# Weight conversion with one integer addition on GpSimd in place of a power of two and a product with it

## The chip, the core and the metric

The kernel runs on one core of a Trainium2 chip. The metric is device time in microseconds (us), from the first to the last instruction, of executions of one fixed program. A core has five engines that each run their own instruction stream in order: TensorE (PE in the rows, its weight loads PEld), VectorE (DVE), ScalarE (ACT), GpSimd (POOL) and SyncE (SP), which here issues DMAs. Semaphores join the streams. An instruction that waits holds up everything behind it in its own stream.

## The reference

Attention with pooled queries (batch 4, 8 heads, 1152 keys, head size 64, pairs of queries averaged to 576), then a layer that mixes with a Fourier transform and has a two-matrix feed-forward part:

```
q_pool = q.reshape(B, H, S // 2, 2, D).mean(axis=3)
attn = softmax(q_pool @ k^T / 8);  x = attn @ v          # heads side by side: [4, 576, 512]
u = x + real(fft(fft(x, axis=1), axis=2))
un = (u - mean(u)) / sqrt(var(u) + 1e-6)
out = u + relu(un @ w_ch1) @ w_ch2                       # w_ch1 512x2048, w_ch2 2048x512
```

The two weight matrices come as float64. The core has no float64 arithmetic, so the kernel turns their bit patterns into float32 itself and splits each weight into a high part that the matmul format (float32r) holds exactly and a low part, the rest. Products are then summed as high x high, low x high and high x low (lines 718 to 720).

## The kernel before, in words

**Attention** goes over 16 pairs of heads, and in each over five blocks of queries, called units here. Lines 229 and 231: scores `s` (TensorE into PSUM) and their scaled copy with a running minimum into `sp` (VectorE). Line 243: exponential (ScalarE). Lines 256 and 259: `sp` transposed by TensorE, and copied out of PSUM to `pt` by ScalarE or, one in five, by VectorE. Line 272: `pt` times the values (TensorE). The next unit's scores are computed between the transposes of this one.

**Heads are prepared** one pair ahead: DMAs of `kr`, `qr`, `vs` from SyncE and of `ks` from GpSimd's queue (line 126), then on GpSimd the sum of query pairs `qr` (195) and the low part of the keys `ks` (198, four pieces), on ScalarE the high part of the queries `qh` (203), and on GpSimd their low part `ql` (206, two or three pieces). The scores of a head need all of these.

**Middle and feed-forward.** When a batch's eight heads are done, its Fourier transform (`dft`) and normalisation (`norm`) run in between, mostly on VectorE and ScalarE. In `norm`, `vt` (587 to 591) is the inverse deviation, `dg` (594) a diagonal of it, and the matmul of line 604 spreads it. `ffn` of a batch runs in blocks of 12 matmuls: four blocks of the first matrix (results `g`, high part on ScalarE in 737, low part on VectorE in 738), then four of the second, four times over. The first batch's blocks fill gaps between the attention's units, and at two places in the program (`drain`) the order demands that they are finished before the attention goes on.

**Weight conversion** is the part that changes. 32 tiles of 128 x 512 float64 are converted once by `convert`, one at a time past the list `inside`: load (SyncE, 643), absolute value of the upper word (ScalarE, 652), clamp (VectorE, 654), shift (VectorE, 656), the lower word scaled (ScalarE, 658), sign and bits joined into `wb` (VectorE, 662), power of two of its exponent (VectorE, 665), high part (ScalarE, 669), then on GpSimd, each in two halves of 128 x 256: lower word times power of two, difference of `wb` and the high part, and their sum as the low part (672). SyncE writes both parts to a DRAM tile (678), from which `wload` fetches them for every batch.

**What sets the order.** There is no scheduler at run time. A planner in the kernel keeps a clock `now`, and every `yield` or `after` says how many nanoseconds later the next step is written into the streams. So the numbers in the `yield`s fix where a step stands among its neighbours.

Of the kernel before, what the change touches and what calls it, by code (L numbers as in the profile page):

```python
# [12 lines left out]
F32 = mybir.dt.float32  # L13
F32R = mybir.dt.float32r
I32 = mybir.dt.int32
U32 = mybir.dt.uint32
AF = mybir.ActivationFunctionType
ALU = mybir.AluOpType
# [6 lines left out]
P = 128  # L25
# [29 lines left out]
def fused_kernel(ctx: ExitStack, tc: tile.TileContext, k2, q2, v2, w1, w2, cst, out):  # L55
    nc = tc.nc
# [10 lines left out]
    cvp = pool("cv", 1)  # L67
# [570 lines left out]
    going = []  # L638

    def convert(f, which):  # L640
        src = (w1, w2)[which]
        w = cvp.tile([P, 512, 2], I32, tag="wraw", name="wraw", bufs=3)
        nc.sync.dma_start(w, src[f].bitcast(I32).rearrange("p (c x) -> p c x", x=2))
        yield 6500 if going else 7000
        while inside:
            yield 400
        inside.append(f)
        high, low = w[:, :, 1], w[:, :, 0]
        a = cvp.tile([P, 512], F32, tag="cv", name="wa", bufs=4)
        ai = a.bitcast(I32)  # L650

        nc.scalar.activation(a, high.bitcast(F32), AF.Abs)
        yield 900 if going else 1400
        nc.vector.tensor_scalar(a, a, WORD_MIN, WORD_MAX, op0=ALU.max, op1=ALU.min)
        yield 700 if going else 1000
        nc.vector.tensor_scalar(ai, ai, 3, 0x3FFFFFF8, op0=ALU.logical_shift_left, op1=ALU.bitwise_and)
        rest = cvp.tile([P, 512], F32, tag="cv", name="rest", bufs=4)
        nc.scalar.activation(rest, low.bitcast(U32), AF.Copy, scale=2.0 ** -52)
        yield 700 if going else 1000
        t = cvp.tile([P, 512], F32, tag="cv", name="wb", bufs=4)  # L660
        b = t.bitcast(I32)
        nc.vector.scalar_tensor_tensor(b, high, -0x40000000, ai, op0=ALU.bitwise_and, op1=ALU.bitwise_or)

        yield 700 if going else 1000
        nc.vector.tensor_scalar(ai, b, -0x800000, None, op0=ALU.bitwise_and)  # L665
        yield 700 if going else 1000
        h = w.rearrange("p c x -> p (c x)").rearrange("p (x c) -> p x c", x=2)
        hi, lo = h[:, 0, :], h[:, 1, :]
        nc.scalar.copy(hi.bitcast(F32R), t)
        for o, x, y, op in ((rest, rest, a, ALU.mult), (t, t, hi.bitcast(F32), ALU.subtract), (lo.bitcast(F32R), t, rest, ALU.add)):  # L670
            for c in (slice(0, 256), slice(256, 512)):
                nc.gpsimd.tensor_tensor(o[:, c], x[:, c], y[:, c], op=op)  # L672
        if not going:
            yield 3000
        inside.pop()
        yield 3000 if going else 1500
        d = scw.tile([P, 2, 512], F32, name=f"w{which}_{f}")
        nc.sync.dma_start(d, h.bitcast(F32))
        wsc[which, f] = d
        yield 6500  # L680
# [7 lines left out]
    def converter():  # L688

        w, f = todo.popleft()  # L690
        g = convert(f, w)
        busy.append(f)

        def go():
            c = next(g, None)
            if c is not None:
                after(c, go)
            else:
                busy.pop()
        go()  # L700
# [257 lines left out]
```

## Time and profile before

| what | value |
|---|---|
| time, median of 3 runs | 1012.21 us (1011.35 to 1012.84) |
| span of the profiled execution | 1012.2 us |
| TensorE busy | 966.5 us (95%) |
| VectorE busy | 601.9 us (59%) |
| ScalarE busy | 526.5 us (52%) |
| GpSimd busy | 402.0 us (40%) |
| mean granted TensorE clock | 0.988 |

The profiled execution's own time is its span, 1012.2 us, the median of the runs to 0.01 us. Busy is the time in which an engine executes something; shares are averages over stages of different limits. The granted clock is the share of TensorE's full clock that the chip allowed, 1.00 for 2.4 GHz and 0.50 for 1.2 GHz.

### The profile page before, as it was taken

To read this page: it belongs to the slowest core of one execution; us is meant where nothing else is said; L and a number is where in the kernel's file an instruction comes from. 1 tells how busy PE (TensorE), PEld (TensorE's weight loads), DVE (VectorE), ACT (ScalarE), POOL (GpSimd) and SP (SyncE) were. 2 spreads that over 40 slices of the span, in tenths; PEclk is the share of its full clock that TensorE was granted. 3 is DMA by queue.
4 is the path that set the end of the run, shared out by engine and by line. 5 is a ranking of instruction groups with operands and counts; after the bars stand their busy time and mean duration, and the time that the engine had idled before them with its cause. 6 is when DMAs were issued, how large, how long until landed. Compare 5 with 4: busy or idle time off the path is not lost.

```text
span 1012.2 us, 19747 instructions
## 1 busy us (share of the span) xinstructions
PE 966.5 (95%) x7398; PEld 840.5 (83%) x7398; DVE 601.9 (59%) x1524; ACT 526.5 (52%) x1033; POOL 402.0 (40%) x583
## 2 busy tenths in 40 slices
PE   8999989898999998998999999999999999999998
PEld 5898878677788887776988888788888888899998
DVE  4557859889875597866544465745644275422222
ACT  5778869658865565655744454535744221301100
POOL 4555776868676667774523222222400000000000
PEclk7999989999999999999999999999999999999999
DMA  6545467556477875485655463254432544744342
GB/s 184 175 128 181 148 200 252 158 167 180 137 241 258 265 242 171 166 313 172 207 187 195 113 207 100 85 177 142 131 121 84 153 147 149 243 133 125 125 125 63
DMA packets 62515, 170.91 MB, mean 169 GB/s; under 512 B 16770, under 2 KB 20242, under 8 KB 62420
## 3 DMA queue, kind: packets, MB, share of 16 engines
q1 hardware_dynamic: 55924, 151.18, 47.1%
q0 software_dynamic: 4320, 17.70, 5.4%
q8 instruction: 58, 0.95, 0.4%
q10 hardware_dynamic: 2176, 0.79, 0.3%
q14 instruction: 37, 0.30, 0.1%
HBM read 146.88 MB, written 22.75 MB: 168 GB/s over the span
## 4 chain that ended last, share of the span: by engine, by line
PE 53%; DVE 2%; ACT 1%; DMA 1%; issue 1%; POOL 1%; SPq 0%; DVEq 0%; ACTq 0%; POOLq 0%
PE f L718 7%; PE f L720 6%; PE f L719 6%; PE s L229 6%; PE o L272 6%; PE t L256 5%; PE t L718 5%; PE t L719 5%; PE t L720 5%; DVE sp L231 1%; DMA w<-w 1%; PE f L532 1%; PE t L532 1%; ACT pt L259 0%; PE f L524 0%
## 5 line engine op out<-in xcount | busy, mean ns | idle before, releaser
L231 DVE TENSOR_SCALAR_CACHE_REDUCE sp<-s,bia 128x384 f32<-128x384 f32 x288 | 177.3, 615 | 89.0 <-PE s L229 66.3
L229 PE MATMUL s<-ks,qh 128*128 128x384 f32 x480 | 185.4, 386 | 12.5 <-DVE sp L231 3.9
L259 ACT COPY pt<-t 128x512 f32<-128x512 f32 (+2 forms) x243 | 125.0, 527 | 111.8 <-PE t L256 110.5
L243 ACT ACTIVATE sp<-sp,bia 128x1152 f32<-128x1152 f32 x144 | 180.1, 1255 | 3.2 <-DVE sp L231 2.8
L229 PE MATMUL s<-ks,ql 128*128 128x384 f32 x480 | 165.1, 344 | 2.9 <-POOL ql L206 2.5
L272 PE MATMUL o<-pt,vs 128*64 128x128 f32 (+1 forms) x2880 | 162.7, 266 | 1.0 <-DVE pt L259 0.8
L272 PEld LDWEIGHTS o<-pt,vs 128*64 128x64 f32 x2880 | 144.5, 138 | 22.8 <-issue 20.5
L256 PE MATMUL t<-ident,sp 128*128 128x128 f32 x1045 | 151.4, 277 | 7.2 <-ACT pt L259 3.0
L256 PEld LDWEIGHTS t<-ident,sp 128*128 128x128 f32 x1045 | 121.5, 141 | 27.8 <-issue 6.3
L198 POOL TENSOR_TENSOR ks<-kr,ks 64x288 fp32r<-64x288 f32 x120 | 99.1, 858 | 57.1 <-DMA ks<-in_k 23.5
L229 PEld LDWEIGHTS s<-ks,qh 128*128 128x128 f32 x480 | 92.6, 193 | 22.5 <-ACT pt L259 6.7
L229 PEld LDWEIGHTS s<-ks,ql 128*128 128x128 f32 x480 | 93.2, 194 | 4.2 <-POOL ql L206 2.9
L737 ACT ACTIVATE g<-f 128x512 fp32r<-128x512 f32 (+1 forms) x49 | 28.2, 576 | 120.2 <-PE f L720 120.2
L738 DVE SCALAR_TENSOR_TENSOR g<-f,g 128x512 fp32r<-128x512 f32 (+1 forms) x49 | 32.5, 663 | 97.1 <-ACT g L737 97.1
L206 POOL TENSOR_TENSOR ql<-qr,qh 128x288 fp32r<-128x288 f32 (+2 forms) x75 | 56.1, 771 | 77.9 <-ACT qh L203 76.8
L231 DVE TENSOR_SCALAR_CACHE_REDUCE sp<-s 128x384 f32<-128x384 f32 x144 | 78.6, 546 | 11.6 <-PE s L229 10.8
L718 PE MATMUL f<-g,w 128*128 128x512 f32 (+1 forms) x192 | 76.0, 396 | 2.0 <-PE f L604 1.0
L718 PE MATMUL f<-unh,w 128*128 128x512 f32 (+1 forms) x196 | 76.7, 391 | 0.9 <-DVE g L738 0.9
L672 POOL TENSOR_TENSOR rest<-rest,wa 128x256 f32<-128x256 f32 x64 | 50.4, 807 | 67.9 <-DVE wa L665 50.8
L720 PE MATMUL f<-unl,w 128*128 128x512 f32 (+1 forms) x196 | 74.6, 380 | 0.0
L719 PE MATMUL f<-unh,w 128*128 128x512 f32 (+1 forms) x196 | 74.3, 379 | 0.0
L720 PE MATMUL f<-g,w 128*128 128x512 f32 (+1 forms) x192 | 74.0, 385 | 0.0
(150 smaller groups left out, 1735.2 us busy)
## 6 DMA issues: line engine op xcount, KB each, us to landing
w<-w SPq DMA_DIRECT2D x128, 512.0 KB, 3.9
qr<-in_q SPq DMA_DIRECT2D x30, 576.0 KB, 4.4
ks<-in_k POOLq DMA_DIRECT2D x30, 576.0 KB, 6.3
wraw<-in_w SPq DMA_DIRECT2D x32, 512.0 KB, 3.5
w<-wraw SPq DMA_DIRECT2D x32, 512.0 KB, 2.6
vs<-in_v SPq DMA_DIRECT2D x32, 288.0 KB, 6.4
kr<-in_k SPq DMA_DIRECT2D x30, 288.0 KB, 6.8
out<-x SPq DMA_DIRECT2D x12, 256.0 KB, 2.0
```

The source lines that it names most:

```text
L198: nc.gpsimd.tensor_tensor(ks[D:, c], kr[D:, c], ks[D:, c].bitcast(F32), op=ALU.subtract)
L206: nc.gpsimd.tensor_tensor(ql[:, z], qr[:, 0, x:y], qh[:, z].bitcast(F32), op=ALU.subtract)
L229: nc.tensor.matmul(ps, lhsT=l, rhs=k, start=i == 0, stop=i == len(ops) - 1)
L231: nc.vector.tensor_scalar(sp[n, j][:, c], ps, -0.0625, bt[:, pc - 1:pc] if pc else None, op0=ALU.mult, op1=ALU.min, accum_out=bt[:, pc:pc ...
L243: last_exp[0] = nc.scalar.activation(t, t, AF.Exp, bias=bia.pop((n, j))[:, 2:3], scale=-1.0, accum_out=den[pr][:, col:col + 1]).ins
L256: nc.tensor.transpose(ps[:, i * P:i * P + P], sp[k][:, c * P:(c + 1) * P], ident)
L259: (nc.vector.tensor_copy if eng == "v" else nc.scalar.copy)(pt[:, :o], ps[:, :o])
L272: nc.tensor.matmul(po[y * D:y * D + D, :w], lhsT=qkv[2 * pr + y][3][:, c, :], rhs=pt[:, o:o + w], start=c == 0, stop=c == NKC - 1)
L672: nc.gpsimd.tensor_tensor(o[:, c], x[:, c], y[:, c], op=op)
L718: nc.tensor.matmul(ps, lhsT=ah, rhs=bh, start=first, stop=False)
L719: nc.tensor.matmul(ps, lhsT=al, rhs=bh, start=False, stop=False)
L720: nc.tensor.matmul(ps, lhsT=ah, rhs=bl, start=False, stop=last)
```

## The change

The rounding to float32 is done on the bit pattern. The lower word, scaled, is converted to an integer `k` by the ScalarE step that used to write `rest`, and GpSimd adds it to the joined bits as a 32-bit integer. So `wb` and `rest` go, with the power of two and with GpSimd's product with it; the difference of the sum and its high part is the low part directly. Per tile GpSimd has four halves in place of six, VectorE three instructions in place of four, ScalarE three as before. ScalarE's copy to the high part now follows a GpSimd instruction, where it followed VectorE's line 662, and the planned distances change.

```diff
         a = cvp.tile([P, 512], F32, tag="cv", name="wa", bufs=4)
+        k = cvp.tile([P, 512], I32, tag="cv", name="wk", bufs=4)
         ai = a.bitcast(I32)
...
-        rest = cvp.tile([P, 512], F32, tag="cv", name="rest", bufs=4)
-        nc.scalar.activation(rest, low.bitcast(U32), AF.Copy, scale=2.0 ** -52)
+        nc.scalar.activation(k, low.bitcast(U32), AF.Copy, scale=2.0 ** -29)
         yield 700 if going else 1000
-        t = cvp.tile([P, 512], F32, tag="cv", name="wb", bufs=4)
-        b = t.bitcast(I32)
-        nc.vector.scalar_tensor_tensor(b, high, -0x40000000, ai, op0=ALU.bitwise_and, op1=ALU.bitwise_or)
-
+        nc.vector.scalar_tensor_tensor(ai, high, -0x40000000, ai, op0=ALU.bitwise_and, op1=ALU.bitwise_or)
         yield 700 if going else 1000
-        nc.vector.tensor_scalar(ai, b, -0x800000, None, op0=ALU.bitwise_and)
-        yield 700 if going else 1000
+        halves = (slice(0, 256), slice(256, 512))
+        for c in halves:
+            nc.gpsimd.tensor_tensor(ai[:, c], ai[:, c], k[:, c], op=ALU.add)
+        yield 2300
         h = w.rearrange("p c x -> p (c x)").rearrange("p (x c) -> p x c", x=2)
         hi, lo = h[:, 0, :], h[:, 1, :]
-        nc.scalar.copy(hi.bitcast(F32R), t)
-        for o, x, y, op in ((rest, rest, a, ALU.mult), (t, t, hi.bitcast(F32), ALU.subtract), (lo.bitcast(F32R), t, rest, ALU.add)):
-            for c in (slice(0, 256), slice(256, 512)):
-                nc.gpsimd.tensor_tensor(o[:, c], x[:, c], y[:, c], op=op)
+        nc.scalar.copy(hi.bitcast(F32R), a)
+        for c in halves:
+            nc.gpsimd.tensor_tensor(lo[:, c].bitcast(F32R), a[:, c], hi[:, c].bitcast(F32R), op=ALU.subtract)
         if not going:
-            yield 3000
+            yield 1000
```

TensorE's stream keeps its order, but for the small matmuls of line 584 in the second batch's `norm`, which stand one feed-forward block (12 matmuls) earlier. The other streams move. Line numbers of the changed program are one or two off from those of before from here on: its 664 is the integer addition, 668 the high part, 670 the difference, 653 the absolute value, 735 the `g` of line 737.

GpSimd's stream where the head pair 8 and 9 is prepared, before; `wa`, `wb`, `rest`, `wraw` belong to the conversion, the others to the heads:

```order
L126 DMA ks<-in_k 128x1152
L672 TENSOR_TENSOR rest<-rest,wa 128x256 x2
L672 TENSOR_TENSOR wb<-wb,wraw 128x256 x2
L672 TENSOR_TENSOR wraw<-wb,rest 128x256 x2
L137 MEMSET qh 128x64
L138 MEMSET ql 128x64
L195 TENSOR_TENSOR qr<-qr 128x288 x2
L198 TENSOR_TENSOR ks<-kr,ks 64x288 x4
```

The same place in the changed program:

```order
L126 DMA ks<-in_k 128x1152
L664 TENSOR_TENSOR wa<-wa,wk 128x256 x2
L137 MEMSET qh 128x64
L138 MEMSET ql 128x64
L195 TENSOR_TENSOR qr<-qr 128x288 x2
L198 TENSOR_TENSOR ks<-kr,ks 64x288 x4
L670 TENSOR_TENSOR wraw<-wa,wraw 128x256 x2
```

Two of the six halves now stand ahead of the head's `qr`, and two behind its `ks`.

ScalarE's stream at the first `drain`, in the second batch's `norm`, before (`vt`, `dg`, `unh` belong to `norm`, `g` to the first batch's feed-forward blocks, `wa`, `rest` and `wraw` to the last conversions):

```order
L652 ACTIVATE wa<-wraw 128x512
L737 ACTIVATE g<-f 128x512
L658 ACTIVATE rest<-wraw 128x512
L737 ACTIVATE g<-f 128x512 x2
L669 CAST wraw<-wb 128x512
L652 ACTIVATE wa<-wraw 128x512
L589 ACT_TABLE_LOAD
L589 ACTIVATE vt<-vt 96x6
L658 ACTIVATE rest<-wraw 128x512
L594 ACTIVATE dg<-ident,vt 96x96 x6
L737 ACTIVATE g<-f 128x512
L669 CAST wraw<-wb 128x512
```

The same place in the changed program:

```order
L658 ACTIVATE wk<-wraw 128x512
L589 ACT_TABLE_LOAD
L589 ACTIVATE vt<-vt 96x6
L594 ACTIVATE dg<-ident,vt 96x96 x6
L668 CAST wraw<-wa 128x512
L653 ACTIVATE wa<-wraw 128x512
L658 ACTIVATE wk<-wraw 128x512
L735 ACTIVATE g<-f 128x512
L668 CAST wraw<-wa 128x512
L653 ACTIVATE wa<-wraw 128x512
L658 ACTIVATE wk<-wraw 128x512
L735 ACTIVATE g<-f 128x512
```

Conversions stand about one tile later against the feed-forward blocks. The last two `g` of this quarter stand, among the rows shown, behind one and two high parts of conversions (668), where they stood behind none and one (669).

## Rows read from the trace of the kernel before

**Rows 1.** Stretch of the conversions: its length, each engine's busy time, granted clock, DMA.

```profile
88.00:475.00 387.00, 354.90 (x2933) 298.80 (x2933) 301.29 (x727) 259.92 (x513) 277.25 (x382) 0.98 0.63 205
```

**Rows 2.** Two stretches at the lower clock, columns PE, PEld, DVE, ACT, POOL, clock, DMA.

```profile
137.20:144.00 6.80, 5.14 (x30) 4.30 (x32) 3.50 (x8) 4.45 (x9) 4.82 (x7) 0.50 0.48 184
181.60:184.90 3.30, 3.30 (x13) 3.13 (x13) 2.75 (x7) 1.05 (x3) 3.30 (x6) 0.50 0.00 0
```

**Rows 3.** Instructions on the tile wa: duration in ns, least, median, most; first and last start.

```profile
L672 POOL TENSOR_TENSOR rest<-rest,wa x64: 719/734/1269, 94.4 to 469.5; 128x256 f32<-128x256 f32 x64
L652 ACT ACTIVATE wa<-wraw x32: 662/676/703, 87.8 to 460.5; 128x512 f32<-128x512 f32 x32
L654 DVE TENSOR_SCALAR wa<-wa x32: 407/667/1075, 90.0 to 462.8; 128x512 f32<-128x512 f32 x32
L656 DVE TENSOR_SCALAR wa<-wa x32: 412/430/1030, 92.7 to 464.4; 128x512 int32<-128x512 int32 x32
L662 DVE SCALAR_TENSOR_TENSOR wb<-wraw,wa x32: 672/691/1296, 93.1 to 466.0; 128x512 int32<-128x512 int32 x32
L665 DVE TENSOR_SCALAR wa<-wb x32: 405/424/1042, 93.9 to 467.9; 128x512 int32<-128x512 int32 x32
```

**Rows 4.** Timeline of POOL and ACT, 118 to 122 us: start, length, what, [idle before].

```profile
118.54 3.28 POOL L198 TENSOR_TENSOR ks<-kr,ks 64x288 fp32r<-64x288 f32 x4 [4.47 <-issue]
119.18 0.60 ACT L669 CAST wraw<-wb 128x512 fp32r<-128x512 f32 x1
121.33 0.59 ACT L259 COPY pt<-f 128x512 f32<-128x512 f32 x1 [0.32 <-PE f L256]
```

**Rows 5.** Timeline of POOL, ACT and PE, 130 to 138 us.

```profile
130.57 1.43 POOL L672 TENSOR_TENSOR rest<-rest,wa 128x256 f32<-128x256 f32 x2
136.43 0.76 ACT L203 CAST qh<-qr 128x512 fp32r<-128x512 f32 x2 [3.59 <-POOL qr L195]
137.90 1.12 PE L256 MATMUL f<-ident,sp 128*128 128x128 f32 x4 [2.80 <-ACT pt L259]
```

**Rows 6.** Timeline of POOL, ACT and PE, 167 to 182 us.

```profile
167.55 0.83 POOL L126 DMA_DIRECT2D ks<-in_k  x1
176.15 3.80 POOL L198 TENSOR_TENSOR ks<-kr,ks 64x288 fp32r<-64x288 f32 x4 [6.02 <-issue]
177.79 0.27 ACT L280 COPY x<-o 128x128 f32<-128x128 f32 x1 [1.95 <-PE o L272]
181.40 0.59 PE L229 MATMUL s<-ks,ql 128*128 128x384 f32 x1 [2.53 <-POOL ql L206]
```

**Rows 7.** Timeline of ACT and PE, 225 to 227 us.

```profile
225.34 0.77 ACT L203 CAST qh<-qr 128x512 fp32r<-128x512 f32 x2 [2.83 <-POOL qr L195]
226.85 0.41 PE L229 MATMUL s<-ks,qh 128*128 128x384 f32 x1 [1.21 <-issue]
```

**Rows 8.** Timeline of POOL, ACT and PE, 374 to 385 us.

```profile
374.69 1.79 POOL L672 TENSOR_TENSOR rest<-rest,wa 128x256 f32<-128x256 f32 x2 [6.27 <-DVE wa L665]
381.90 0.76 ACT L203 CAST qh<-qr 128x512 fp32r<-128x512 f32 x2 [4.41 <-POOL qr L195]
384.41 0.44 PE L256 MATMUL t<-ident,sp 128*128 128x128 f32 x2 [2.23 <-ACT pt L259]
```

**Rows 9.** Timeline of DVE and PE, 245 to 248 us.

```profile
245.43 0.91 DVE L665 TENSOR_SCALAR wa<-wb 128x512 int32<-128x512 int32 x1
247.89 0.44 PE L229 MATMUL s<-ks,qh 128*128 128x384 f32 x1 [2.54 <-DVE sp L231]
```

**Rows 10.** Timeline of ACT, DVE and PE at the first drain, 436 to 461 us.

```profile
436.43 0.67 ACT L652 ACTIVATE wa<-wraw 128x512 f32<-128x512 f32 x1 [5.68 <-DMA wraw<-in_w]
453.93 0.15 DVE L587 TENSOR_SCALAR vt<-f 96x6 f32<-96x6 f32 x1
459.29 0.75 PE L604 MATMUL f<-dg,onesm 96*128 96x288 f32 x2 [1.25 <-DVE g L738]
461.00 0.47 PE L718 MATMUL f<-g,w 128*128 128x512 f32 x1 [0.95 <-PE f L604]
```

## The prediction

> **What bounds the kernel now.** I read the page first: TensorE is busy 95% of the span, and the chain of waits that ended last is mostly TensorE. So a change elsewhere can only move TensorE's idle time and its clock. Then the busy time by stretches, for the stretch in which weights are converted: in 387.0 us TensorE works 354.9, VectorE 301.3, POOL 277.3, ScalarE 259.9 [rows 1]. The most to be had there is thus 387.0 - 354.9 = 32.1 us, besides the clock. The first conversion starts at 87.8 and the last at 460.5 [rows 3]; behind them nothing but the order of a few instructions changes, and TensorE's stream is the same, so what is won or lost by then is passed on to the end. Third, TensorE's timeline with its waits: the 32 us lie in many gaps, and five of 1.2 to 2.8 us carry the argument. For each I looked at the streams of the engine it waits for, one step further back.
>
> In four of them the end of the chain is GpSimd, because six halves of a conversion stand ahead of a head's work. At 137.90 TensorE has waited 2.80 us for ScalarE, which had waited 3.59 us for `qr` on GpSimd, which came behind conversion halves that began at 130.57 [rows 5]. At 181.40 it has waited 2.53 us for `ql`; GpSimd was late since `ks` came 8.6 us after its DMA, and that DMA's issue stood behind a conversion until 167.55 [rows 6]. At 226.85 and 384.41 the pattern of 137.90 repeats, with 1.21 and 2.23 us [rows 7, 8]. The fifth, 2.54 us at 247.89, is VectorE's: a power of two of 0.91 us stands just ahead of the score copy that TensorE needs [rows 9]. The first two are also followed by the lower clock, 0.50 for 6.8 and 3.3 us, in which TensorE worked 5.14 and 3.30 us [rows 2].
>
> **The change part by part, removed work.** GpSimd loses 64 of 192 halves of 0.734 us, 47 us, and VectorE 32 powers of two of 0.424 us, 13.6 us [rows 3]. Little of that lies on TensorE's path; it counts where a gap stands.
>
> *Gap at 137.90.* Four halves of this conversion leave the place ahead of `qr`: 4 x 0.734 = 2.9 us, so `qh` could start near 133.5 in place of 136.43 [rows 5]. Against it stands a new wait earlier. The conversion before has its addition behind `ks`, which ends at 118.54 + 3.28 = 121.82 [rows 4]; the addition then ends near 123.3. ScalarE's high part, which ran at 119.18 for 0.60 us, now stands just ahead of the copy of 121.33 and waits for it, so that copy starts near 123.9 less the 0.6 us that its old place gives back: 2.0 us lost. ScalarE, free at 136.43 - 3.59 = 132.84 before, then comes to `qh` near 132.84 + 2.0 and with hand-overs at 135.2, behind GpSimd's 133.5. Net of both: 136.43 - 135.2, 1.2 us won.
>
> *Gap at 181.40.* GpSimd reaches the DMA of `ks` at least 2.9 us earlier (four halves), which covers the 2.53 us. But the high part now stands ahead of the copy of 177.79 and needs an addition that is queued behind `ql`; ScalarE was idle 1.95 us there [rows 6], so I take 1.0 us of new wait. Net 1.5 us.
>
> *The clock.* If neither gap is long, neither fall comes: half of 5.14 and half of 3.30 us, 2.6 and 1.6 [rows 2]. The first place keeps some idle time from the new wait, so I take 2.0 there. Together 3.6 us, from 0 to 4.2.
>
> *Gaps at 226.85 and 384.41.* At the second, GpSimd's idle 6.27 us for the power of two is over too, since its conversion now stands behind the head's `ql` [rows 8]. I take both whole: 1.2 + 2.2 = 3.4 us.
>
> *VectorE.* The power of two stood ahead of a score copy at 247.89, 0.9 us [rows 9]; for all its other places I count its usual 0.424 once [rows 3]: 1.3 us. Its 0.91 in place of 0.424 was a collision. The Trainium skill (SBUF — State Buffer, Who interferes with whom) has VectorE and GpSimd lock one pair of ports for a whole instruction, so that the loser blocks. The trace agrees, the shift ran 412 to 1030 ns [rows 3]. By that rule fewer GpSimd halves would free other VectorE steps too, and this term would be nearer 2 us and the sum below 0.7 lower; as heads' halves fill GpSimd's place there, I leave it at 1.3.
>
> **New instructions.** ScalarE's conversion to an integer takes the place of one step of its kind and counts nothing; ScalarE works 259.9 of 387 us, so a tenth of a microsecond more is covered, and without that cover 32 x 0.1 is 3 us. The trace has no integer addition on GpSimd. Below stands the float half, 719 ns at its fastest, above the slowest, 1269 [rows 3]. I take the median, 0.734, as it reads and writes operands of the same number and size as the float half that it replaces. The Trainium skill (GPSIMD Engine Reference, Elementwise — side-by-side cycle accounting) puts the floor of a two-input operation at its read port, about 2.6 cycles an element, which for 256 elements with its dispatch comes to an estimate of 0.71 us whatever the operation. By that the rival on the slow addition would hardly exist; no run here has shown it, so it keeps a chance.
>
> **The drain, where the change costs.** Before, conversions ran one tile ahead of the feed-forward blocks; now the last ones stand among the `g` and the normalisation [order rows of ScalarE]. The line: the sign step of one conversion stands in VectorE's stream behind 587, which ended at 454.08 [rows 10]. With ScalarE's 5.68 us wait for a weight load gone (the conversion concerned now comes later) and line 584 a block earlier, that end comes up to 2 us sooner, 452. From there, in order and each waiting for the one before: sign 0.69, addition 2 x 0.734, high part 0.60, then a loop of absolute value 0.68, clamp 0.67, shift 0.43, sign 0.69, addition 1.47, high part 0.60, then once more 0.68 + 0.67 + 0.43 + 0.69, and the low part of the last `g`, some 0.69 [rows 3, 4]. That is 2.76 + 4.54 + 2.47 + 0.69 = 10.5, and with about 0.1 for each of some ten hand-overs 11.5: 463.5. The same `g` released TensorE's line 604 at 459.29 before [rows 10], so the block that began at 461.00 begins 4.2 us later. What is behind: TensorE itself, with blocks and attention; nothing gives it back. From below 1.5 us, if only one loop is exposed; from above 9, if a third loop and another fall of the clock come on top.
>
> **Sum.** 1.2 + 1.5 + 3.6 + 3.4 + 1.3 = 11.0 us won. Where a gap closes, the next late engine often holds a part of it; VectorE is busy 301 of 387 us. I leave a quarter, and win 8.2. Less 4.2: 4.0. From 1012.2 that is **1008.2**, and the profiled execution is the median of the runs.
>
> **The rivals.**
> *Gaps refill.* VectorE at 78% is just behind, so half or less is won and the drain takes it: 5 - 4.2, about 1011.5. For it speaks that VectorE ends gaps of its own; against, that four of the gaps are plainly GpSimd's.
> *The drain decides (slower).* A further loop of 4.5 us is exposed, since the block's weights, written only behind the difference, come late as well, and the longer idle time brings a fall of the clock: 4.2 + 4.5 + 0.6, 9.3 lost against 6 won: 1015.5. It decides from where the block of 461.00 loses more than the 8.2 won ahead of it. For it speaks that conversions now stand a tile later; against, that two of the loops overlap TensorE's block of 2.7 us.
> *A slow addition (slower).* At 1269 ns a half, each loop in the drain and each of the two new ScalarE waits grows by 1.1 us: 2 x 1.1 and some 2.2 with it, 4 to 5 us, and the gains shrink by a like part: 1014. It decides from about 1.2 us a half.
> *All gaps close and the drain costs little.* 11.0 less 1.5: 1002.7.
>
> **How the numbers follow.** Forecast 0.44, gaps refill 0.18, the drain decides 0.16, a slow addition 0.07, all close 0.15. Changes under 0.2%, 2 us, can't be told from none. Faster by more: all of "all close", nearly all of the forecast and little of the refill, 0.60. Same: most of the refill and an edge of the forecast, 0.18. Slower: 0.22. The range, 1000 to 1015, holds "all close" with some room and the slow addition, and cuts the drain's rival in half. The forecast's own range is 1004 to 1010.
>
> **What would show it.** Right: in the profile after, GpSimd busy some 47 us less, VectorE some 14; no wait of ScalarE for `qr` over 2 us near 135, 225 and 380; `ks` DMA of the gap at 181 issued 3 us or more earlier; clock 1.00 there; an idle stretch of TensorE at the drain ahead of lines 604 and 718 longer by some 4 us. Wrong: an integer half well over 0.74 us; ScalarE waiting for the addition in more than three or four places; gaps of the old size with VectorE named.

## The result, and the profile after

The changed kernel takes 1002.75 us (median of 4 runs, 1001.70 to 1006.21) against 1012.27 us on the same chip: a ratio of 0.9908, 95% interval 0.9887 to 0.9928, so 9 us faster. Timed again, beside the experiments, it took 1005.44 us (6 runs, 1000.56 to 1006.23), ratio 0.9911, 0.9892 to 0.9930. The forecast was 1008.2 with a range of 1000 to 1015: right in direction and range, with a gain of 4 forecast where 9 came. The first profiled execution, with a span of 999.9 us, is one of the shortest of these runs; the second, 1003.8 us, lies nearer to the median. The experiments are compared with 1005.44. Both profiles are read below, because what differs between them turned out to be a cost of the change. In every run from here on the time is 1.7 to 2.1 us above the span. By that measure the profiled execution of the kernel before, with a span of 1012.2 us, took some 1014 us; it is then not the median of the first runs, as the section on before says, but near that of the later ones (1013.3 to 1014.0). The differences of starts below are taken against it.

From the page of the changed kernel: busy time, share of the span and instructions of each engine.

```profile
PE 965.2 (97%) x7398; PEld 840.3 (84%) x7398; DVE 578.7 (58%) x1492; ACT 527.0 (53%) x1033; POOL 351.8 (35%) x519
```

Busy time in the stretch of the conversions, to be held against [rows 1]; columns as there.

```profile
88.00:475.00 387.00, 365.60 (x3070) 309.05 (x3070) 286.06 (x720) 269.68 (x531) 229.69 (x322) 0.98 0.66 212
```

GpSimd (POOL) does 50.2 us less (402.0 before) and VectorE (DVE) 23.2 less, where 47 and 13.6 were forecast from medians. By sums the 32 powers of two took 16.6 us (0.52 on the mean), and the three steps that VectorE keeps take 6.1 us less than before: the clamp 2.8, the shift 1.9 and the sign step 1.5. TensorE works 365.6 of the 387 us, so in this execution its idle time there fell from 32.1 to 21.4 us. The mean granted clock of the stretch is 0.98, as before. The instructions on the tile wa, duration least, median, most:

```profile
L664 POOL TENSOR_TENSOR wa<-wa,wk x64: 713/728/1256, 93.4 to 455.2; 128x256 int32<-128x256 int32 x64
L670 POOL TENSOR_TENSOR wraw<-wa,wraw x64: 719/733/1244, 96.8 to 457.4; 128x256 fp32r<-128x256 f32 x64
L655 DVE TENSOR_SCALAR wa<-wa x32: 408/465/998, 89.3 to 450.5; 128x512 f32<-128x512 f32 x32
L660 DVE SCALAR_TENSOR_TENSOR wa<-wraw,wa x32: 672/690/1182, 92.4 to 453.7; 128x512 int32<-128x512 int32 x32
L668 ACT CAST wraw<-wa x32: 602/618/632, 96.1 to 456.0; 128x512 fp32r<-128x512 f32 x32
```

The integer half takes 0.728 us where 0.734 was taken: the rival of a slow addition is dead at once. That the prediction's estimate of 0.71 us comes close is luck: it added a dispatch time that is not GpSimd's. The Trainium skill (GPSIMD Engine Reference, Elementwise — side-by-side cycle accounting) gives a dispatch of about 156 ns for VectorE only; its 2.6 cycles an element for a two-input addition on GpSimd alone come, at 1.2 GHz, to an estimate of 0.55 us for 256 elements. The measured 0.728 us lies above that.

To see where the time went, I matched TensorE's instructions before and after by their count among those on the same tiles and took the start after minus the start before, in us. A column is an instruction, named by its start before; a negative number says how far the kernel is ahead there. First and second are the two executions of the changed kernel, the rest are the experiments below (late_3500 is late_early_3500).

```
start before   119.9 145.4 174.6 182.5 186.9 201.8 226.9 247.9 265.3 345.2 384.6 441.5 461.0 466.1   end
first            0.2  -5.4  -6.1  -8.7  -9.0  -9.9 -11.6 -14.3 -10.9 -12.8 -14.9 -16.7 -12.5 -12.2 -12.3
second           0.6  -4.5  -5.7  -7.7  -2.4  -4.4  -6.2  -7.5  -7.1  -8.9 -11.0 -12.8  -8.6  -8.4  -8.4
no_product      -1.2  -5.4  -6.0  -6.9  -6.6  -8.4  -9.4  -9.5  -9.6  -9.5 -11.8 -13.7 -13.7 -14.2 -13.7
six_halves      -0.8  -5.5  -5.0  -7.6  -4.0  -6.1  -7.6  -9.7  -5.7  -6.5  -8.2 -10.1  -5.4  -5.2  -5.3
power_back       0.9  -5.0  -4.6  -7.2  -6.4  -7.3  -8.7  -9.4  -7.3  -8.5 -10.9 -13.2  -7.5  -7.6  -7.5
split_order      0.8  -3.7   2.2  -0.9  -1.3  -2.4  -3.8  -3.6  -1.5  -2.6  -3.7  -2.1   5.8   5.1   9.0
short_drain      0.3  -5.0  -6.0  -8.6  -6.5  -8.6 -10.3 -12.0  -9.8 -11.0 -13.8 -15.4 -15.6 -16.4 -15.8
own_high        -0.8  -5.6  -6.4  -8.9  -9.2 -10.1 -11.8 -14.1 -12.0 -13.7 -16.5 -19.3 -15.9 -14.0 -11.9
late_high       -2.4  -8.8  -7.5  -9.8 -10.1 -10.2 -12.0 -14.5 -13.9 -14.9 -17.1 -19.0  -5.5  -3.2  -0.5
late_early      -0.0  -6.0  -2.0  -5.1  -1.7  -3.9  -5.7  -5.6  -2.6  -3.9  -7.3  -8.4 -12.6 -10.8  -8.3
late_3500       -0.3  -6.2  -5.3  -7.8  -3.7  -5.4  -7.1  -7.5  -4.2  -6.1  -9.0  -9.9 -13.9 -11.9 -10.6
short_own       -0.3  -5.6  -6.0  -8.6  -8.8  -9.8 -11.5 -13.3 -12.8 -13.7 -16.5 -19.1 -19.2 -20.1 -19.6
pool_high        0.0  -4.2  -4.6  -7.1  -7.4  -7.3  -9.0 -10.7 -10.5 -12.3 -14.8 -17.8 -17.7 -18.9 -18.9
```

In the first two lines: up to the drain 16.7 and 12.8 us are won, in many places; from 441.5 to 461.0 4.2 are given back, in both. The two executions part between 182.5 and 186.9, by 5.6 us; 3.0 of these come back by 265.3, where the first execution loses 3.4 us and the second 0.4.

**The place of 137.90 [rows 5].** Timeline of the changed kernel (first execution; POOL, ACT and PE), 110 to 137 us:

```profile
110.17 0.57 POOL L126 DMA_DIRECT2D ks<-in_k  x1
114.75 3.72 POOL L198 TENSOR_TENSOR ks<-kr,ks 64x288 fp32r<-64x288 f32 x4 [2.24 <-issue]
118.55 1.41 POOL L664 TENSOR_TENSOR wa<-wa,wk 128x256 int32<-128x256 int32 x2
...
121.02 0.63 ACT L668 CAST wraw<-wa 128x512 fp32r<-128x512 f32 x1
132.43 0.61 ACT L668 CAST wraw<-wa 128x512 fp32r<-128x512 f32 x1
132.93 0.77 ACT L203 CAST qh<-qr 128x512 fp32r<-128x512 f32 x2
...
136.44 0.44 PE L256 MATMUL f<-ident,sp 128*128 128x128 f32 x2 [0.69 <-ACT pt L259]
```

The 2.80 us of idle TensorE are 0.69, and ScalarE's copy of `qh` starts at 132.93 in place of 136.43, without its wait. The new wait that I put at 121 is not there: `ks` starts at 114.75, 3.8 us before its place in [rows 4], so the addition ends at 119.96, before ScalarE comes to its high part at 121.02.

**The place of 181.40 [rows 6].** Here the new wait came. The first execution (POOL, ACT and PE):

```profile
168.51 2.61 POOL L206 TENSOR_TENSOR ql<-qr,qh 128x288 fp32r<-128x288 f32 x3
171.09 1.93 POOL L664 TENSOR_TENSOR wa<-wa,wk 128x256 int32<-128x256 int32 x2
173.05 0.62 ACT L668 CAST wraw<-wa 128x512 fp32r<-128x512 f32 x1 [2.69 <-POOL wa L664]
174.94 0.44 PE L229 MATMUL s<-ks,qh 128*128 128x384 f32 x1 [0.56 <-ACT pt L259]
```

and the second:

```profile
168.49 4.67 POOL L198 TENSOR_TENSOR ks<-kr,ks 64x288 fp32r<-64x288 f32 x4 [4.55 <-DMA ks<-in_k]
173.25 2.44 POOL L206 TENSOR_TENSOR ql<-qr,qh 128x288 fp32r<-128x288 f32 x3
175.65 1.62 POOL L664 TENSOR_TENSOR wa<-wa,wk 128x256 int32<-128x256 int32 x2
177.30 0.62 ACT L668 CAST wraw<-wa 128x512 fp32r<-128x512 f32 x1 [6.18 <-POOL wa L664]
179.17 0.69 PE L229 MATMUL s<-ks,qh 128*128 128x384 f32 x1 [3.75 <-ACT pt L259]
```

with its busy time by a stretch, columns as in [rows 2]:

```profile
175.00:185.00 10.00, 6.25 (x52) 5.29 (x51) 7.03 (x21) 5.95 (x13) 5.05 (x9) 0.66 0.49 155
```

The chain reads from top to bottom: GpSimd waits 4.55 us for the DMA of `ks`; `ql` and then the addition stand behind; ScalarE's high part waits 6.18 us for the addition, and the copies of `pt` that stand behind it on ScalarE come late for TensorE, which idles 3.75 us and is then granted the lower level, 1.2 GHz. In the first execution `ql` starts 4.7 us earlier and the same chain costs 0.56 us, with no fall of the clock. That is the 5.6 us by which the two part here, and about the spread of the runs. The DMA of `ks` was issued at 156.22 in the first execution and at 158.30 in the second, and `ks` began 8.0 and 10.2 us later: half of the difference is the issue, half the way from there.

**The clock.** The two falls of before, at 137.2 and 181.5, are gone in the first execution, but others came, at 238.6, 436.5 and 446.8 (columns as in [rows 2]):

```profile
238.60:242.00 3.40, 3.37 (x26) 2.93 (x28) 2.02 (x6) 3.38 (x7) 3.40 (x5) 0.50 0.58 178
436.50:439.90 3.40, 3.40 (x10) 2.62 (x9) 0.42 (x2) 3.28 (x9) 2.41 (x4) 0.51 0.75 298
446.80:453.60 6.80, 6.46 (x14) 4.30 (x14) 6.73 (x11) 4.40 (x7) 2.68 (x4) 0.50 0.72 243
```

Before, the falls at 137.2, 181.5 and 461.4 put TensorE at the lower level for 13.6 us between 88 and 475 us. In the first execution after it is 13.6 us again, and in the second too (from 178.2 and from 447.9). The falls moved; they did not become fewer in time.

**The drain [rows 10].** PE, first execution:

```profile
434.98 0.64 PE L584 MATMUL f<-onesm,sq 128*96 128x1 f32 x6 [1.44 <-DVE sq L579]
442.65 0.65 PE L604 MATMUL f<-dg,onesm 96*128 96x288 f32 x2
447.10 1.33 PE L604 MATMUL f<-dg,onesm 96*128 96x288 f32 x2 [3.80 <-DVE g L736]
448.47 0.76 PE L716 MATMUL f<-g,w 128*128 128x512 f32 x1
```

and its busy time by a stretch:

```profile
446.00:454.00 8.00, 6.80 (x15) 4.43 (x16) 7.93 (x13) 4.40 (x7) 2.90 (x4) 0.57 0.77 271
```

The second pair of line 604 waits 3.80 us for the low part of the last `g`, as forecast, where it waited 1.25; then the lower clock (0.57 on the mean of 8 us). The block that began at 461.00 begins at 448.47. The two ends of the prediction's chain, on VectorE:

```profile
435.66 0.16 DVE L587 TENSOR_SCALAR vt<-f 96x6 f32<-96x6 f32 x1 [0.49 <-PE f L584]
446.36 0.68 DVE L736 SCALAR_TENSOR_TENSOR g<-f,g 128x512 fp32r<-128x512 f32 x1
```

From the end of 587 to the end of that `g` it takes 11.2 us, where 11.5 were forecast.

### The profile page after: what moved, and what is told of

Its sections match the earlier page's. It is cut to its first block, busy times and chain, and to the rows that moved or that the text cites. A ratio compares the mean times of both kernels' runs of the same rounds, so it can differ in the third digit from the quotient of the medians.

```text
span 999.9 us, 19669 instructions
## 1 busy us (share of the span) xinstructions
PE 965.2 (97%) x7398; PEld 840.3 (84%) x7398; DVE 578.7 (58%) x1492; ACT 527.0 (53%) x1033; POOL 351.8 (35%) x519
## 4 chain that ended last, share of the span: by engine, by line
PE 83%; DVE 7%; ACT 5%; POOL 2%; issue 2%; DMA 1%; DVEq 0%; ACTq 0%; POOLq 0%
PE s L229 14%; PE o L272 13%; PE t L256 10%; PE f L716 9%; PE f L718 8%; PE f L717 8%; PE t L716 5%; PE t L718 5%; PE t L717 5%; PE f L256 3%; DVE sp L231 2%; PE f L532 2%; ACT pt L259 1%; ACT sp L243 1%; PE f L524 1%
## 5 line engine op out<-in xcount | busy, mean ns | idle before, releaser
L229 PEld LDWEIGHTS s<-ks,qh 128*128 128x128 f32 x480 | 91.9, 191 | 16.7 <-DVE sp L231 5.1
L664 POOL TENSOR_TENSOR wa<-wa,wk 128x256 int32<-128x256 int32 x64 | 47.9, 767 | 84.5 <-DVE wa L660 62.0
```

The lines of the kernel that those rows point to most:

```text
L229: nc.tensor.matmul(ps, lhsT=l, rhs=k, start=i == 0, stop=i == len(ops) - 1)
L664: nc.gpsimd.tensor_tensor(ai[:, c], ai[:, c], k[:, c], op=ALU.add)
```

## The experiments

My theory after the result: the gain comes from the two halves that GpSimd no longer does in each conversion, and the drain gives 4 us back. Rivals: the gain comes from the new order (the conversion in two pieces, with the DMA for `ks` ahead of the second); it comes from VectorE's missing power of two; what costs is not the order in the drain but ScalarE's wait for the addition. The kernel before was timed beside them in four rounds and took 1013.3 to 1014.0 us.

**The changed kernel again (after_again).**

> The changed kernel itself once more, beside the others on one chip. Both theories: 1001 to 1005 us; the first profile, 999.9 us, was among the fastest executions, so a profile a few us longer is likely, with a fall of the clock more or at another place.

1005.44 us, ratio 0.9911 (0.9892 to 0.9930). Its profile is the second execution above; its lower clock from 178.2 stands behind the new wait.

**Two halves put back (six_halves).**

```diff
         nc.scalar.copy(hi.bitcast(F32R), a)
+        for c in halves:
+            nc.gpsimd.tensor_tensor(lo[:, c].bitcast(F32R), a[:, c], a[:, c], op=ALU.add)
         for c in halves:
             nc.gpsimd.tensor_tensor(lo[:, c].bitcast(F32R), a[:, c], hi[:, c].bitcast(F32R), op=ALU.subtract)
```

> The changed kernel with two additional GpSimd halves in each conversion (they write the low part, which the difference then overwrites, so the result is the same); every engine's order is else that of the changed kernel. Theory (GpSimd's load ahead of the heads made the gaps): GpSimd busy again near 400 us, the waits for qr, ks and ql come back, with at least one fall of the clock more before the drain, and the drain's loops grow by 1.5 us each: 1009 to 1016 us. Rival (the new order with its two pieces did it, not the number of halves): 1001 to 1005 us, as the changed kernel.

1008.65 us, ratio 0.9951 (0.9938 to 0.9965): 3.2 slower than the changed kernel, just under the range of my theory and above the rival's. Two reasons can be given for the small size. The first shows in its profile: a half that reads one source twice is shorter, so that GpSimd is busy 391.3 us, not 402. The second is by its edit: both halves were put into the second piece, which at 137.90 stands behind `qr`; no run prices that alone.

```profile
L670 POOL TENSOR_TENSOR wraw<-wa x64: 602/613/1169, 94.8 to 464.1; 128x256 fp32r<-128x256 f32 x64
```

The place of 137.90 keeps its gain (-0.8 to -5.5 in the table), though six halves are back: there the order is enough. Fewer halves in the old order are enough too (no_product, -1.2 to -5.4).

**The power of two put back (power_back)**; its output is overwritten later.

```diff
         nc.vector.scalar_tensor_tensor(ai, high, -0x40000000, ai, op0=ALU.bitwise_and, op1=ALU.bitwise_or)
+        lo = w.rearrange("p c x -> p (c x)").rearrange("p (x c) -> p x c", x=2)[:, 1, :]
+        nc.vector.tensor_scalar(lo, ai, -0x800000, None, op0=ALU.bitwise_and)
```

> The changed kernel with the power of two's instruction put back on VectorE (it writes where the low part will be written later, so the result is the same). Theory (VectorE's share is one or two places, 1.3 us in the prediction): 1003.5 to 1006 us. Rival (VectorE was the engine just behind TensorE, and its 13 us less made most of the gain): 1008 to 1012 us, with gaps of TensorE that end with VectorE.

1006.26 us, ratio 0.9934 (0.9915 to 0.9952): 0.8 above the changed kernel, and the intervals overlap. VectorE's share is small; the 1.3 us of the prediction are neither confirmed nor excluded. The rival's 1008 to 1012 is not met by the median, though the interval's upper end, 1009.1, reaches into it.

**The product taken out of the kernel before (no_product)**; the low words are added unscaled.

```diff
-        for o, x, y, op in ((rest, rest, a, ALU.mult), (t, t, hi.bitcast(F32), ALU.subtract), (lo.bitcast(F32R), t, rest, ALU.add)):
+        for o, x, y, op in ((t, t, hi.bitcast(F32), ALU.subtract), (lo.bitcast(F32R), t, rest, ALU.add)):
```

> The kernel before without the product's two GpSimd halves in each conversion: the low words are added unscaled, so the conversion's result is not the reference's; power of two, order and planned distances are those of the kernel before. Theory (fewer halves ahead of the heads): the gaps at 137.9, 181.4, 226.9 and 384.4 go, no new wait of ScalarE comes and the drain loses nothing: 998 to 1004 us. Rival (the new order did it): 1010 to 1013 us.

1000.64 us, ratio 0.9875 (0.9857 to 0.9892): 13.3 us won with fewer halves alone, in the old order. The drain costs nothing: the table shows -13.7 on both sides of it. The lower clock is down to one fall, 3.4 us from 175.7. One gap that the expectation called gone stayed, 2.04 us for `ql` at 174.92.

**Six halves in the order of the changed kernel (split_order).**

```diff
         nc.vector.tensor_scalar(ai, b, -0x800000, None, op0=ALU.bitwise_and)
-        yield 700 if going else 1000
+        halves = (slice(0, 256), slice(256, 512))
+        for c in halves:
+            nc.gpsimd.tensor_tensor(rest[:, c], rest[:, c], a[:, c], op=ALU.mult)
+        yield 2300
...
-        for o, x, y, op in ((rest, rest, a, ALU.mult), (t, t, hi.bitcast(F32), ALU.subtract), (lo.bitcast(F32R), t, rest, ALU.add)):
+        for o, x, y, op in ((t, t, hi.bitcast(F32), ALU.subtract), (lo.bitcast(F32R), t, rest, ALU.add)):
...
-            yield 3000
+            yield 1000
```

> The arithmetic of the kernel before (six halves, power of two) in the order and planned distances of the changed kernel: the product stands where the addition does, then the distance of 2300, then high part, difference and sum. Theory (the fewer halves bring the gain, the order costs some of it): the addition's kernel with two extra halves ran 1008.7 and the power of two cost 0.8, and the real halves are a little longer, so 1009 to 1014 us. Rival (the order, above all GpSimd's DMA for ks ahead of the second piece, brings the gain): 1003 to 1007 us.

1024.21 us, ratio 1.0097 (1.0066 to 1.0128): slower than before by 10.9, and above even my theory's range. With the three others this makes a square, all with the power of two:

```
                 old order            order of the change
six halves       1013.3 to 1014.0     1024.2 (split_order)
four halves      1000.6 (no_product)  1006.3 (power_back)
```

Two halves fewer win 13 us in the old order and 18 in the new; the new order loses 5.6 with four halves and 10.9 with six. So the rival is refuted for the whole, though at 137.90 the order is enough: from 119.9 to 145.4 this kernel gains 4.5 us like the others. The square is not pure: in split_order ScalarE's high part does not wait for GpSimd, and 5.9 of its lost us lie from 145.4 to 174.6, around the long copy on VectorE that the last section shows. In the drain it waits 6.01 us at line 604, which fits longer conversions there costing more, as the prediction's slow addition would have.

**The drain in its old order (short_drain).**

```diff
-        yield 2300
+        yield 700 if going else 2300
```

> The changed kernel with a planned distance of 700 in place of 2300 behind the addition once the feed-forward runs; a conversion then ends where it did before, and the drain's rows stand again as in the kernel before. Theory (conversions that stand later lose 4 us in the drain): the idle 3.8 to 4.1 us ahead of the line 604 go back to about 1.3, with no fall of the clock there: 1000 to 1003 us, against 1005.4. Rival (what costs in the drain is the chain through the addition itself, wherever it stands): 1004 to 1006 us.

1000.18 us, ratio 0.9850 (0.9826 to 0.9874): 5.3 less than the changed kernel. In its profile the wait at line 604 is that of [rows 10] again:

```profile
443.98 0.75 PE L604 MATMUL f<-dg,onesm 96*128 96x288 f32 x2 [1.25 <-DVE g L736]
```

Nothing is lost between 441.5 and 461.0. A short fall of the clock stayed there, 3.4 us from 445.7, against the expectation.

**ScalarE freed from the addition (own_high)**; the high part is copied from ScalarE's own integer tile, so high and low parts are not the reference's.

```diff
-        nc.scalar.copy(hi.bitcast(F32R), a)
+        nc.scalar.copy(hi.bitcast(F32R), k.bitcast(F32))
```

> The changed kernel, but ScalarE's high part is copied from ScalarE's own integer tile and not from the sum, so that ScalarE never waits for GpSimd's addition (the high parts are then not those of the reference); every engine's order stays. Theory (ScalarE's new waits cost at 175 to 179 us, where one of 6.2 us held TensorE for 3.8 and a fall of the clock followed, and in the drain): 998 to 1002 us. Rival (these waits are covered by others): 1004 to 1006 us.

1000.96 us, ratio 0.9871 (0.9848 to 0.9894): 4.5 less, with intervals that just touch. It wins at the place of 181.40, where the table goes on to -9.2 in place of the second execution's -2.4 (the first, with the shorter wait, stood at -9.0 too), and next to nothing in the drain, which still gives back 3.4 up to 461.0 and 7.4 up to the end (a further fall of the clock, 3.4 us from 453.2, lies there). So the wait for the addition costs in the first half, in executions like the second, and the order costs in the drain.

**The high part later, in the first half (late_high).**

```diff
-        yield 2300
+        yield 2300 if going else 4500
```

> The changed kernel with a planned distance of 4500 in place of 2300 behind the addition before the feed-forward runs (2300 after that): the high part stands later in ScalarE's stream. Theory (the wait for the addition is one of order in the first half): no wait of ScalarE over 2 us for the addition near 175, one fall of the clock less: 1001 to 1004 us. Rival (a later high part makes the next conversion and the weights late and moves the waits elsewhere): 1005 to 1008 us.

1013.52 us, ratio 0.9996 (0.9983 to 1.0008): my theory fell. The wait near 175 did go (-10.1 at 186.9), and TensorE stood 19.0 us ahead at 441.5, but then 18.5 were lost. Timeline of PE at its drain:

```profile
448.19 0.77 PE L716 MATMUL f<-unh,w 128*128 128x512 f32 x1 [7.51 <-DMA w<-w]
...
462.95 0.77 PE L716 MATMUL f<-g,w 128*128 128x512 f32 x1 [4.49 <-DMA w<-w]
```

TensorE waits for weights that were converted too late. This is what the prediction's rival "the drain decides" describes, in a kernel that puts the conversions off further.

**The same, with an early start of the next conversion (late_early).**

```diff
-        yield 2300
+        inside.pop()
+        yield 700 if going else 4500
...
-        inside.pop()
```

> Three distances of the changed kernel at once: the high part 4500 behind the addition before the feed-forward runs and 700 after that, and the next conversion may begin as soon as the addition is issued, so that conversions don't come later in the drain than in the kernel before. Theory (the late high part gains up to the drain, where the kernel with 4500 alone stood 8 to 12 us ahead of the changed kernel, and it lost that to weights that came late): 991 to 997 us. Rival (what the late high part gained before the drain came from conversions that were put off into the drain, and comes back as load when they stand early): 999 to 1004 us.

1004.55 us, ratio 0.9913 (0.9895 to 0.9931). With 3500 in place of 4500:

> As the kernel with 4500 and 700 and the early release, with 3500 in place of 4500; the last conversions stand still a block earlier. Theory: 992 to 998 us, and within 3 us of the other, since both take the conversions out of the drain. Rival: 999 to 1004 us.

1003.40 us, ratio 0.9901 (0.9881 to 0.9922). The second lies in the rival's range, the first half a us above it, and both far from the theory's. The drain now gains, but the lead ahead of it is smaller. With 4500 the kernel stands 2.0 ahead at 174.6 in place of 6, behind waits of 2.33 and 2.77 us for ScalarE's `pt`; with 3500 the loss comes between 182.5 and 186.9, behind a wait of 3.74 for the same. That fits work that had been put off and comes back, but three distances changed at once, and no run separates them. From late_early:

```profile
164.73 0.69 PE L229 MATMUL s<-ks,qh 128*128 128x384 f32 x1 [2.33 <-ACT pt L259]
180.79 0.44 PE L229 MATMUL s<-ks,qh 128*128 128x384 f32 x1 [2.77 <-ACT pt L259]
```

**Both single edits (short_own).** The distance of `short_drain` and the copy of `own_high` together (high and low parts as there).

> Both single edits at once: the distance of 700 in place of 2300 once the feed-forward runs, and the high part taken from ScalarE's own integer tile, so that ScalarE never waits for the addition (the high parts are not those of the reference). Theory (the drain's order and ScalarE's wait near 175 us are two separate costs of 5 and 4.4 us): 995 to 998 us, no gap over 2 us at either place. Rival (one cost seen twice): 999 to 1001 us, as either edit alone.

994.21 us, ratio 0.9804 (0.9788 to 0.9821): 11.2 less than the changed kernel, where the two alone won 5.3 and 4.5. They are two costs, and not one seen twice. The lower clock is down to 3.4 us.

**A version for use (pool_high).** The high part moves to GpSimd, which made the sum, and the drain's distance is short.

```diff
-        yield 2300
+        yield 700 if going else 2300
...
-        nc.scalar.copy(hi.bitcast(F32R), a)
+        for c in halves:
+            nc.gpsimd.tensor_copy(hi[:, c].bitcast(F32R), a[:, c])
```

> The distance of 700 once the feed-forward runs, and the high part copied on GpSimd in two halves and not on ScalarE, so that the whole tail of a conversion is on one engine; the result is the reference's. Theory (ScalarE's wait near 175 goes, 4.4 us won, but two extra halves on GpSimd cost about the 3.2 that they cost before): 997 to 1002 us. Rival (GpSimd's load decides alone): 1003 us or more.

995.75 us, ratio 0.9819 (0.9797 to 0.9841): faster than both kernels and than expected. The added halves are short, 0.40 us each. From its instructions on wa and its busy time by stretches:

```profile
L669 POOL CAST wraw<-wa x64: 388/399/930, 95.0 to 450.6; 128x256 fp32r<-128x256 f32 x64
88.00:475.00 387.00, 365.62 (x3141) 310.63 (x3141) 291.82 (x735) 259.50 (x510) 257.77 (x392) 1.00 0.67 213
```

GpSimd works 257.8 us there, 28 more than in the changed kernel, and the whole is faster all the same; ScalarE works 10 less, and the granted clock is 1.00 over the whole stretch, with no fall in it.

## Why the prediction was right in direction and too small

**The mechanism held.** Fewer halves on GpSimd ahead of a head's `qr`, `ks` and `ql` close TensorE's gaps; no_product shows 13.3 us for that alone. The drain's chain, its place and its size held as well: the block of 461.00 loses 4.2 us between 441.5 and 461.0, forecast 4.2, and short_drain takes it back by the distance alone. That the size fits to a tenth is in part luck. The prediction counted both additions as steps of the chain; in the first execution the first of them ended at 437.99, while ScalarE was busy with `dg` until 438.32, and own_high, where ScalarE waits for neither, still loses 3.4. So the additions are worth some 0.8 of the 4.2; the rest is that the conversions stand there.

**The step that failed is the sum before the drain**, "I leave a quarter, and win 8.2": 16.7 and 12.8 us were won there. By terms, from the table (first, second execution; a place holds its idle time and its clock together):

- Gap at 137.90 with its clock, from 119.9 to 145.4: 5.6 and 5.1, forecast 1.2 + 2.0. The 2.0 lost to a new wait at 121 did not come: I had counted the earlier issue of the DMA for `ks` at 181 but not here, though its issue stood behind a conversion here too. It moved from 111.71 to 110.17, by 1.5 us, and `ks` by 3.8; the other 2.3 are a shorter way from issue to start, for which no run shows the reason. This term was mis-sized.
- Gap at 181.40 with its clock, from 145.4 to 186.9: 3.6 won, and 2.1 lost; forecast 1.5 + 1.6. ScalarE's wait there, 1.95 before and forecast at 1.0 more, was 2.69 and 6.18. The order showed the wait; its size hangs on when a DMA is issued and lands, which one execution cannot tell.
- Gap at 226.85, from 201.8: 1.7 and 1.8, forecast 1.2 (the row of [rows 7] names no releaser, so that the pattern of 137.90 repeats there was read into it). Gap at 384.41, from 345.2: 2.1 and 2.1, forecast 2.2.
- VectorE, at 247.89: 2.7 and 1.3, forecast 1.3; by 265.3, 3.4 and 0.4 were given back, in the first execution with the new fall of the clock at 238.6. power_back puts the whole of the power of two at 0.8, within its interval. That other VectorE steps would be freed too came true, by the 6.1 us above; what they are worth no run shows.
- Not in the sum at all: 186.9 to 201.8 (0.9 and 2.0), 265.3 to 345.2 (1.9 and 1.8) and 384.6 to 441.5 (1.8 and 1.8), 4.6 and 5.6 together. The prediction took five gaps and put the others at nothing (1.40 us at 201.14 and 1.39 at 437.62 among them in the trace of before).

The five named places, with what was given back by 265.3, won 12.3 and 7.8 us, where 11.0 were summed and 8.2 left. So the quarter that was taken off was needless in the first execution and about right in the second; what is missing in both is the 5 us of the places that the sum left out. That these smaller gaps have the same cause is likely, since no_product wins 13.3 us, but no run follows them one by one.

**The clock's term** of 3.6 us was right at the two places and wrong for the whole: the lower level was granted for 13.6 us before and after. Half of TensorE's busy time in it is 6.0 us before, 6.6 and 4.7 after, so by this measure the clock lost 0.6 us in the one and won 1.3 in the other. What was won is idle time in the main: over the same instructions, those from 88.0 to 475.0 before, TensorE was idle for 32.1 us before and for 21.1 and 27.6 after.

**One sign of being wrong came**: ScalarE waits for the addition in eight places, more than "three or four", in the first execution between 88 and 475 us (in total, times, longest):

```profile
ACT wraw L668 <- POOL wa L664: 14.3, 8, 3.4
```

It says little by itself: that execution still won 12.3 us in all, and own_high, without these waits, won 11.9 by the table. The other signs: no wait of ScalarE for `qr` over 2 us in the conversions, and the DMA of `ks` at 156.22 and 158.30 in place of 167.55.

**The rivals.** Gaps refill: in part true at one place, 181.40, and only in some executions. The drain decides: not in this kernel, but late_high shows it, with 7.51 and 4.49 us for weights. A slow addition: refuted by 0.728 us. All gaps close and the drain costs little: its 1002.7 is the time measured, by luck: more was won and the drain did cost 4.

## What to carry to other kernels

A stage that is split in two so that one engine waits for another in the middle has two prices, and each can be tested alone: the instructions that queue behind the waiting one, and the planned distance that pushes all later work towards the drain. Here removing the work was worth 13 us and the order that came with it cost 5 to 6 of them, until the distance was shortened and the middle step moved to the engine that had just made its input. A sum over the few largest gaps understates a gain that lies in many: the small ones were worth 5 us here. And a fall of the clock that goes at one place can come at another, so its gain is counted over the whole stretch, not at the place.

## What the runs showed of the hardware

A one-row copy on VectorE took ten times its usual time while GpSimd ran almost without a pause. In split_order, VectorE and then GpSimd, 162 to 167 us:

```profile
162.38 4.74 DVE L462 COPY tmp<-x 1x576 f32<-1x576 f32 x1
162.37 1.42 POOL L675 TENSOR_TENSOR wb<-wb,wraw 128x256 f32<-128x256 f32 x2
163.74 1.39 POOL L675 TENSOR_TENSOR wraw<-wb,rest 128x256 fp32r<-128x256 f32 x2
165.08 0.14 POOL L137 MEMSET qh<- 128x64 f32 x1
...
165.27 1.53 POOL L195 TENSOR_TENSOR qr<-qr 128x288 f32<-128x288 f32 x2
```

Its median in the same kernel is 0.45 us. GpSimd's row of instructions ends at 166.80, the copy at 167.12, and TensorE waited 4.42 us for the score copy behind it. The DMA engines were fully busy in that stretch too (share 1.03), but the traces separate the two. Of the 168 one-row copies of this kind in the 14 traces, 40 took over 0.5 us; each of these began while a GpSimd instruction ran and ended 0.31 to 0.32 us after the end of one. All 93 during which GpSimd did nothing took 0.43 to 0.45 us, with the DMA share up to 1.13. And this one, in split_order, took twice its usual time with no DMA at all (the last line has its stretch, columns as in [rows 1]):

```profile
354.71 2.00 POOL L206 TENSOR_TENSOR ql<-qr,qh 128x288 fp32r<-128x288 f32 x2
356.09 0.95 DVE L459 COPY tmp<-x 1x576 f32<-1x576 f32 x1
356.09:357.04 0.95, 0.95 (x6) 0.78 (x5) 0.95 (x1) 0.00 (x0) 0.63 (x1) 1.00 0.00 0
```

So it was GpSimd that held the copies up. The Trainium skill (SBUF — State Buffer, Who interferes with whom) has the two engines share one pair of ports under an exclusive lock that one instruction holds to its end; the traces agree with that, and the copy at 162.38 would then have missed eight turns in a row.

On GpSimd, a half with two sources took 0.73 us, one that reads a source twice 0.61, a copy 0.40; the integer addition took what float halves do (0.728 against 0.734 and 0.733).
